# A mixture-of-experts kernel on one core: second-layer products on two row tiles

## The chip, the cores and the metric

The kernel runs on one core of a Trainium2 chip. Its time is the device time of one execution in microseconds. Before the change the median of three timed runs is 708.6 us (708.54 to 709.06).

## What is computed

The reference has two parts. The first is linear attention over 8 batches, 8 heads and 576 positions: features are exp(p) and exp(−p) of a projection less its largest magnitude, and out = (q · (k v)) / (q · z). The second part takes the attention's output as x, 4608 tokens of 512 numbers, and sends each token to one of 8 experts:

```python
for each token s of batch b, in order:
    fresh_e = argmax(logits[b, s])
    e = fresh_e if s == 0 or local_gate[b, s] < 0.5 else prev_e
    prev_e = e
    h = np.maximum(x[b, s] @ w1[e], 0.0)        # 512 -> 1024
    out[b, s] = p[e] * (h @ w2[e])              # 1024 -> 512, p is the softmax of the logits
```

Which expert gets which token is known only on the chip, so the kernel makes lists of tokens there.

## The kernel before, in words

The attention and the gates fill the first 280 us or so. What follows is the experts' work, in *slots*. A slot is one expert's weights and up to four *units* of 128 tokens. The order of the slots is fixed in `moe` and `slots`: two early slots of three units each, and then, from about 347 us, slots of four and of three units in turn (four of each), with one *two-expert slot* after the first two, then a slot of two units, and last the *late* slot, which again has two experts. A two-expert slot is one unit whose 128 rows are 64 tokens of one expert and 64 of another. In some slots the last unit is short (96 tokens); which ones is fixed too.

A slot has two layers. `layer1` multiplies the weights with x, 512 to 1024, for all the units at once, eight blocks of 128 features, each in four products over 128 inputs; ScalarE's ReLU writes `hh` and VectorE the remainder `hl` (L1433, L1434). `layer2` then goes unit by unit: eight blocks `f` of 128 features are the 128 rows of the contraction, the unit's tokens are the stationary operand and 512 columns of w2 stream past.

Numbers are split in two for the one-pass format fp32r: a high part and the low remainder, for the weights (`whi`, `wlo`: `split`, a cast on ScalarE at L1208 and a subtraction on VectorE at L1211) and for the activations. A product of two such numbers is three matmuls, high by high, high by low, low by high (`three`, L1387 to L1389). "A product" below is one such matmul: a unit's second layer has 8 × 3 = 24 of them, all added in one PSUM bank, tile `l2`, which has two buffers. Two-expert slots go through the other branch of `both` (L1400), which uses plain fp32 and two 128x64 column tiles, one for each expert.

When a unit is done, VectorE scales its rows by the gate's probability (L1499; ScalarE does it in the early slots, L1497) into `y`, which has two buffers, and POOL scatters the rows to the output with an indirect DMA (L1503, `put`). The late slot is finished by `last_rows`, in two parts of the columns. `halfbanks` gives the two-bank tile into which a two-expert slot turns rows (L1369); of two such tiles one was in the pool of `l2` with a name of its own, the other in a pool beside it.

The instructions of each engine stand in the order in which the program issues them, TensorE's exactly in the written order. While `layer2` runs, calls from `between` and `used`/`spare` issue the next slot's work between the blocks: weights are loaded by SyncE, split by ScalarE and VectorE, and the next x is turned and split into high and low parts. Splits of weights stand behind the last marked instruction of their engine (`past`, `marks`), and the scaling of a unit sets such a mark.

Of the kernel before, what the change touches and what calls it, by code (L numbers as in the profile page):

```python
# [7 lines left out]
F32 = mybir.dt.float32  # L8
# [5 lines left out]
ALU = mybir.AluOpType  # L14
# [5 lines left out]
DM, E, FF = 512, 8, 1024  # L20
# [46 lines left out]
class Kernel:  # L67
# [236 lines left out]
    def paced_load(self, at, behind):  # L304

        if self.loads and NBP * NHP * NC - 12 - len(self.loads) < at - 4:
            with self.tc.issue_after(behind.ins):
                self.loads.pop(0)()
# [958 lines left out]
    def halfbanks(self):  # L1267

        self.trn = getattr(self, "trn", 0) + 1
        return (self.psr if self.trn % 2 else self.pst).tile([128, 2, 512], F32, name="tr", bufs=1)  # L1270

    def into(self, s):
        if "x" not in s:
# [117 lines left out]
    def both(self, s, k, o, ah, al, c, first, last):  # L1391
# [6 lines left out]
        for z in (0, 1):  # L1398
            r = slice(64 * z, 64 * z + 64)
            self.last_pe = self.pe.matmul(o[r], ah.bitcast(F32)[:, r], w[z][:, c], start=first, stop=last)  # L1400

    def behind(self):

        x, self.last_num = self.last_num, None
        return self.tc.issue_after(x.ins) if x else nullcontext()
# [64 lines left out]
    def layer2(self, s, between, held=None):  # L1470
        dve = self.dve
        hh, hl = s["h"]
        self.need(s, 8) if len(s["ei"]) == 1 else None
        if held is not None:
            return self.last_rows(s, between, held)
        for k in range(s["n"]):
            if hasattr(self, "psr"):
                t = self.psr.tile([128, DM], F32, name="l2")
            else:
                t = self.psb.tile([128, DM], F32, name="l2", tag="nm")  # L1480
            o = self.unit(s, k)
            t = t[0:o.stop - o.start]
            for f in range(8):
                c = slice((f % 2) * DM, (f % 2) * DM + DM)
                self.both(s, 4 + f // 2, t, hh[:, f, o], hl[:, f, o], c, f == 0, f == 7)
                if f in ((0, 2) if s["n"] > 1 else (1, 3, 5)) and between:
                    between.pop(0)()
                if f % 2 and k == s["n"] - 1:
                    self.used(1)
                elif f % 2:  # L1490
                    self.spare()
            rows = slice(0, o.stop - o.start)
            y = self.mx2.tile([128, DM], F32, name="y")[rows]
            u = s["u"] + k
            prob = s["prob"][rows, u:u + 1]
            if s in self.eslots:
                self.marks[self.act] = self.act.mul(y, t, prob)  # L1497
            else:
                self.marks[dve] = dve.tensor_scalar_mul(y, t, prob)  # L1499
            self.put(y, s["tok"][rows, u:u + 1])  # L1500

    def put(self, y, at):
# [5 lines left out]
    def last_rows(self, s, between, held):  # L1508

        hh, hl = s["h"]  # L1510
        y = self.mx2.tile([128, DM], F32, name="y")
        u = s["u"]
        prob = s["prob"][:, u:u + 1]
        for a, b in ((0, WIDE), (WIDE, DM)):
            t = self.psr.tile([128, DM], F32, name="l2")[:, 0:b - a]
            for f in range(8):
                c = slice((f % 2) * DM + a, (f % 2) * DM + b)
                self.both(s, 4 + f // 2, t, hh[:, f], hl[:, f], c, f == 0, f == 7)
            self.marks[self.act] = self.act.mul(y[:, a:b], t, prob)
        self.used(4)  # L1520
        held.append(lambda at=s["tok"][:, u:u + 1]: self.put(y, at))
# [174 lines left out]
```

## Time and profile before

| | |
|---|---|
| median of the timed runs | 708.6 us |
| the profiled execution's own time | 705.87 us |
| its span, first to last instruction | 704.1 us |
| instructions in the trace | 21968 |
| TensorE busy | 696.7 us (99%) |
| TensorE loading weights (beside its matmuls) | 615.7 us (87%) |
| VectorE busy | 475.7 us (68%) |
| ScalarE busy | 351.0 us (50%) |
| POOL busy | 236.4 us (34%) |

Busy time is the union of the rows' durations. A matmul's end is modelled and matmuls overlap, so the pace of TensorE is read from the starts of rows that follow each other, and not from their durations. The profiled execution is one execution; the timed runs are others. In a row, `128*128` is the part of the array that is used (rows by columns), and `128x512` the streamed operand.

### The profile page before, as it was taken

What the parts mean: (1) busy time and instruction counts of PE and PEld (TensorE: products, weight loads), DVE (VectorE), ACT (ScalarE), POOL (GpSimd) and SP (SyncE); (2) the same over time, 40 slices, a digit from 0 to 9 for tenths busy, and PEclk for the clock granted to TensorE, in tenths of its full rate; (3) what the DMA queues carried; (4) which work ended last, traced back from release to release, by engine and by line L of the source; (5) the groups of instructions that cost most, each with busy time, mean ns of one, the idle gap of its engine ahead of it and who ended that gap; (6) DMA issues with size and microseconds to landing.
All of it is one profiled execution on the core that took longest, in us unless ns stands there. A gap on an engine that the chain in (4) does not pass through costs nothing. (4 is left out here: it accounts for less than half of the span.)

```text
span 704.1 us, 21968 instructions
## 1 busy us (share of the span) xinstructions
PE 696.7 (99%) x9193; PEld 615.7 (87%) x9193; DVE 475.7 (68%) x878; ACT 351.0 (50%) x696; POOL 236.4 (34%) x349
## 2 busy tenths in 40 slices
PE   8999999999999999999999999999999999999997
PEld 7999999999999999889888975889888997889894
DVE  6888899889998986694538348455756466644610
ACT  6667676766778884243534226342425143424320
POOL 0211101420257674665606053042523225140201
PEclk9999999999999999999999999999999999999999
DMA  8855545554578843254887998736866686646611
GB/s 241 257 159 151 160 129 147 150 148 138 143 226 247 265 142 92 56 192 147 281 190 256 343 331 316 165 143 173 216 184 186 193 185 215 152 148 154 242 55 41
DMA packets 100885, 129.51 MB, mean 184 GB/s; under 512 B 41682, under 2 KB 80018, under 8 KB 100734
## 3 DMA queue, kind: packets, MB, share of 16 engines
q1 hardware_dynamic: 92304, 105.10, 51.9%
q0 software_dynamic: 8032, 22.78, 9.7%
q8 instruction: 73, 1.20, 0.7%
q14 instruction: 28, 0.23, 0.1%
q10 hardware_dynamic: 448, 0.20, 0.1%
HBM read 98.12 MB, written 21.80 MB: 170 GB/s over the span
## 5 line engine op out<-in xcount | busy, mean ns | idle before, releaser
L1433 ACT ACTIVATE hh<-l 128x384 fp32r<-128x384 f32 (+4 forms) x88 | 45.0, 511 | 163.2 <-PE l L1389 163.0
L1387 PE MATMUL l<-xhi,whi 128*128 128x352 f32 (+5 forms) x352 | 124.2, 353 | 0.0
L1389 PE MATMUL l<-xhi,wlo 128*128 128x352 f32 (+5 forms) x352 | 123.6, 351 | 0.0
L1388 PE MATMUL l<-xlo,whi 128*128 128x352 f32 (+5 forms) x352 | 123.4, 351 | 0.0
L1434 DVE SCALAR_TENSOR_TENSOR hl<-l,hh 128x384 fp32r<-128x384 f32 (+4 forms) x88 | 51.0, 580 | 100.3 <-ACT hh L1433 100.2
L1211 DVE TENSOR_TENSOR wlo<-wraw,whi 128x1024 fp32r<-128x1024 f32 x80 | 101.8, 1289 | 23.2 <-ACT whi L1208 23.0
L1387 PE MATMUL l<-whi,hh 128*128 128x512 f32 (+1 forms) x288 | 112.7, 391 | 0.0
L1388 PE MATMUL l<-wlo,hh 128*128 128x512 f32 (+1 forms) x288 | 112.3, 390 | 0.0
L1389 PE MATMUL l<-whi,hl 128*128 128x512 f32 (+1 forms) x288 | 112.3, 390 | 0.0
L420 ACT ACTIVATE kp<-sb 128x512 f32<-128x512 f32 x140 | 81.1, 624 | 41.0 <-DVE sb L412 39.7
L410 DVE TENSOR_REDUCE m<-pj 128x8 f32<-128x1024 f32 x70 | 85.4, 1221 | 16.6 <-PE pj L407 12.9
L1208 ACT CAST whi<-wraw 128x1024 fp32r<-128x1024 f32 x80 | 82.0, 1045 | 18.4 <-PE l L1389 12.7
L412 DVE TENSOR_TENSOR sb<-pj,m 128x1024 f32<-128x1024 f32 x70 | 85.7, 1225 | 6.2 <-DVE m L410 0.5
L538 PE MATMUL nm<-kvs,qp 128*64 128x74 f32 x2304 | 86.9, 227 | 0.0
L407 PE MATMUL pj<-first,kq 64*128 64x128 f32 x1120 | 81.3, 285 | 0.3 <-ACT ks L508 0.3
L538 PEld LDWEIGHTS nm<-kvs,qp 128*64 128x64 f32 x2304 | 79.6, 136 | 0.4 <-issue 0.3
L443 ACT ACTIVATE qp<-pj 128x512 f32<-128x512 f32 x140 | 76.4, 597 | 6.6 <-PE pj L428 6.2
L460 PE MATMUL kvp<-v,kp 128*64 128x65 f32 x2048 | 77.1, 225 | 0.1
L1503 POOL DMA_INDIRECT out<-y,p_tokm x32 | 40.5, 1267 | 104.5 <-DVE y L1499 93.7
L407 PEld LDWEIGHTS pj<-first,kq 64*128 64x128 f32 x1120 | 67.9, 187 | 6.1 <-ACT ks L508 0.5
L1387 PEld LDWEIGHTS l<-xhi,whi 128*128 128x128 f32 x352 | 66.1, 188 | 6.7 <-issue 0.8
L1388 PEld LDWEIGHTS l<-xlo,whi 128*128 128x128 f32 x352 | 66.2, 188 | 5.4
(269 smaller groups left out, 977.0 us busy)
## 6 DMA issues: line engine op xcount, KB each, us to landing
wraw<-in_w1h SPq DMA_DIRECT2D x40, 512.0 KB
wraw<-in_w2h SPq DMA_DIRECT2D x40, 512.0 KB
kq<-in_kqT SPq DMA_DIRECT2D x88, 192.0 KB
v<-in_va SPq DMA_DIRECT2D x48, 195.0 KB
xs<-xo SPq DMA_DIRECT2D x48, 128.0 KB
whi<-in_w2h SPq DMA_DIRECT2D x8, 512.0 KB
wlo<-in_w2h SPq DMA_DIRECT2D x8, 512.0 KB
xs<-xo SPq DMA_DIRECT2D x16, 192.0 KB
```

The costliest lines, as they stand in the source:

```text
L407: self.last_pe = self.pe.matmul(t[:, h, i % 2, j, :], kq[r, j, s], self.w2[r], start=True, stop=True)
L410: dve.tensor_reduce(m, f, AX.X, ALU.max, apply_absolute_value=True)
L412: self.last_dve = dve.tensor_sub(sb.rearrange("p h c j f -> p (h c j) f"), f, m.unsqueeze(2).broadcast_to([128, 8, 128]))
L420: self.last_act = act.activation(kp[:, :, :, sg, :].rearrange("p c h f -> p h c f"), sb[:, :, :, 0], AF.Exp, scale=1.0 - 2 * sg)
L443: self.act.activation(qp[:, sg].rearrange("p h (c r k) -> p (h c) r k", c=2, r=2), src, AF.Exp, scale=1.0 - 2 * sg)
L460: self.last_sum = self.pe.matmul(t[r, sg, h], kp[:, h, sg, r], v[:, h], start=first and sg + h == 0, stop=last and sg + h == 2)
L538: self.last_num = self.pe.matmul(e["t"][r, c - c0, k], self.ch[i]["qp"][:, sg, h, q0 + r.start:q0 + r.stop], kvs[:, sg, k], start=sg == 0, ...
L1208: self.act.copy(hi, raw)
L1211: (low or self.dve).tensor_sub(lo[:, c], raw[:, c], hi.bitcast(F32)[:, c])
L1387: mm(o, ah, bh, start=first, stop=False)
L1388: mm(o, ah, bl, start=False, stop=False)
L1389: self.last_pe = mm(o, al, bh, start=False, stop=last)
```

## The change

The second layer of each slot with one expert, from the point where the late pools are open (so not in the two early slots), is computed by `row_tiles`. Each matmul of 128 rows becomes two of 64 rows: the lower half of the contraction goes to the first bank of a pair and the upper half to the second. The two banks of the pair are added when the rows are scaled: ScalarE multiplies the first bank by the probability into `y`, and VectorE multiplies the second and adds `y`. The tile `l2` is therefore two banks wide, still with two buffers, and the turn tile of `halfbanks` that stood in the same pool becomes one of these buffers. Two-expert slots use the first bank of such a tile and VectorE's scaling as before.

```diff
     def halfbanks(self):
         self.trn = getattr(self, "trn", 0) + 1
-        return (self.psr if self.trn % 2 else self.pst).tile([128, 2, 512], F32, name="tr", bufs=1)
+        if self.trn % 2:
+            return self.psr.tile([128, 2, 512], F32, name="l2")
+        return self.pst.tile([128, 2, 512], F32, name="tr", bufs=1)
...
+    def row_tiles(self, s, k, t, ah, al, c, first, last):
+
+        wh, wl = s["w"][k]
+        for a, b in ((ah, wh), (ah, wl), (al, wh)):
+            for r in (0, 1):
+                p = slice(64 * r, 64 * r + 64)
+                self.last_pe = self.pe.matmul(t[:, r], a[p], b[p, c], start=first and b is wh and a is ah,
+                                              stop=last and a is al)
...
         for k in range(s["n"]):
-            if hasattr(self, "psr"):
-                t = self.psr.tile([128, DM], F32, name="l2")
+            rest = hasattr(self, "psr")
+            split = rest and len(s["ei"]) == 1
+            o = self.unit(s, k)
+            rows = slice(0, o.stop - o.start)
+            if rest:
+                t = self.psr.tile([128, 2, DM], F32, name="l2")[rows]
             else:
-                t = self.psb.tile([128, DM], F32, name="l2", tag="nm")
-            o = self.unit(s, k)
-            t = t[0:o.stop - o.start]
+                t = self.psb.tile([128, 1, DM], F32, name="l2", tag="nm")[rows]
             for f in range(8):
                 c = slice((f % 2) * DM, (f % 2) * DM + DM)
-                self.both(s, 4 + f // 2, t, hh[:, f, o], hl[:, f, o], c, f == 0, f == 7)
+                if split:
+                    self.row_tiles(s, 4 + f // 2, t, hh[:, f, o], hl[:, f, o], c, f == 0, f == 7)
+                else:
+                    self.both(s, 4 + f // 2, t[:, 0], hh[:, f, o], hl[:, f, o], c, f == 0, f == 7)
...
-            if s in self.eslots:
-                self.marks[self.act] = self.act.mul(y, t, prob)
+            if split:
+                self.marks[self.act] = self.act.mul(y, t[:, 0], prob)
+                self.marks[dve] = dve.scalar_tensor_tensor(y, t[:, 1], prob, y, ALU.mult, ALU.add)
+            elif s in self.eslots:
+                self.marks[self.act] = self.act.mul(y, t[:, 0], prob)
             else:
-                self.marks[dve] = dve.tensor_scalar_mul(y, t, prob)
+                self.marks[dve] = dve.tensor_scalar_mul(y, t[:, 0], prob)
             self.put(y, s["tok"][rows, u:u + 1])
...
-            t = self.psr.tile([128, DM], F32, name="l2")[:, 0:b - a]
+            t = self.psr.tile([128, 2, DM], F32, name="l2")[:, 0, 0:b - a]
```

## Rows read from the trace of the kernel before

**Rows 1.** The page: busy us, share and instructions by engine; granted clock in 40 slices.

```profile
PE 696.7 (99%) x9193; PEld 615.7 (87%) x9193; DVE 475.7 (68%) x878; ACT 351.0 (50%) x696; POOL 236.4 (34%) x349
...
PEclk9999999999999999999999999999999999999999
```

**Rows 2.** Busy time by stage: the slots after the early ones; one second layer.

```profile
core 0: us, PE busy (x) PEld busy (x) DVE busy (x) ACT busy (x) POOL busy (x), PEclk, DMA share, GB/s
346.94:691.86 344.92, 344.92 (x1698) 290.08 (x1696) 186.99 (x226) 123.95 (x190) 101.64 (x84) 1.00 0.69 202
...
458.42:480.18 21.76, 21.76 (x98) 18.02 (x96) 13.55 (x15) 7.09 (x9) 9.96 (x8) 1.00 0.40 131
```

**Rows 3.** Timeline, second layer of four full units: start us, us, engine, line, operation.

```profile
458.42 0.39 PE L1387 MATMUL l<-whi,hh 128*128 128x512 f32 x1
...
478.14 0.39 PE L1387 MATMUL l<-whi,hh 128*128 128x512 f32 x1
478.14 0.19 PEld L1388 LDWEIGHTS l<-wlo,hh 128*128 128x128 f32 x1
...
480.18 0.32 PE L1387 MATMUL l<-xhi,whi 128*128 128x352 f32 x1
```

**Rows 4.** Timeline, first layer of the two-unit slot, 96 products, to the next layer.

```profile
666.78 0.30 PE L1387 MATMUL l<-xhi,whi 128*128 128x320 f32 x1
...
680.86 0.39 PE L1387 MATMUL l<-whi,hh 128*128 128x512 f32 x1
```

**Rows 5.** Timeline, a short unit's 24 products, between a full unit and the next slot.

```profile
506.30 0.39 PE L1389 MATMUL l<-whi,hl 128*128 128x512 f32 x1
506.53 0.39 PE L1387 MATMUL l<-whi,hh 128*96 128x512 f32 x1
...
512.05 0.39 PE L1387 MATMUL l<-xhi,whi 128*128 128x512 f32 x1
```

**Rows 6.** Groups by line and shape: the scaling (xcount | busy us, mean ns | idle before).

```profile
L1499 DVE TENSOR_SCALAR y<-l,p_probm 128x512 f32<-128x512 f32 x27 | 20.1, 746 | 37.8 <-PE l L1389 37.8
...
L1499 DVE TENSOR_SCALAR y<-l,p_probm 96x512 f32<-96x512 f32 x4 | 3.0, 740 | 1.5 <-DMA out<-y,p_tokm 1.5
```

**Rows 7.** Timeline, the attention's plain fp32 row tiles: twelve matmuls and the next.

```profile
102.75 0.84 PE L407 MATMUL pj<-first,kq 64*128 64x128 f32 x12
103.42 0.22 PE L428 MATMUL pj<-first,sb 64*128 64x64 f32 x1
```

**Rows 8.** Timeline, TensorE into and out of the two-expert slot's column tiles.

```profile
421.14 0.40 PE L1389 MATMUL l<-whi,hl 128*96 128x512 f32 x1
421.47 0.43 PE L1400 MATMUL l<-whi,xhi 128*64 128x256 f32 x1
...
435.52 0.59 PE L1400 MATMUL l<-whi,hh 128*64 128x512 f32 x1
...
435.95 0.59 PE L1400 MATMUL l<-whi,hh 128*64 128x512 f32 x1
...
436.48 0.50 PE L1387 MATMUL l<-xhi,whi 128*128 128x512 f32 x1
```

**Rows 9.** Groups by line and shape: weight splits, ReLU remainder, early slots' scaling.

```profile
L1211 DVE TENSOR_TENSOR wlo<-wraw,whi 128x1024 fp32r<-128x1024 f32 x80 | 101.8, 1289 | 23.2 <-ACT whi L1208 23.0
L1208 ACT CAST whi<-wraw 128x1024 fp32r<-128x1024 f32 x80 | 82.0, 1045 | 18.4 <-PE l L1389 12.7 <-DMA wraw<-in_w2h 2.8 <-DMA wraw<-in_w1h 2.8
L1434 DVE SCALAR_TENSOR_TENSOR hl<-l,hh 128x512 fp32r<-128x512 f32 x24 | 16.6, 692 | 32.0 <-ACT hh L1433 32.0
L1497 ACT ACTIVATE y<-l,p_probe 128x512 f32<-128x512 f32 x6 | 4.1, 686 | 7.1 <-PE l L1389 4.8 <-issue 2.3
```

**Rows 10.** Who waited for whom: us in total, times, longest.

```profile
POOL out L1503 <- DVE y L1499: 93.7, 17, 18.6
```

**Rows 11.** Timeline, the last scaling before the late slot, and the last scatter.

```profile
691.96 0.75 DVE L1499 TENSOR_SCALAR y<-l,p_probm 128x512 f32<-128x512 f32 x1 [4.69 <-PE l L1389]
...
699.67 0.97 POOL L1503 DMA_INDIRECT out<-y,p_tokm  x1 [5.71 <-ACT y L1519]
```

More of the change, by code (lines that the diff above doesn't have):

```diff
@@ L1491, in layer2 @@
                     self.spare()
-            rows = slice(0, o.stop - o.start)
             y = self.mx2.tile([128, DM], F32, name="y")[rows]
```

## The prediction

> **What bounds the kernel now.** I read the page first, then the busy times by stage, then single matmuls in order of time. The page shows TensorE busy for 99% of the span, at the full granted clock (the 2.4 GHz level) in all 40 slices [rows 1]. An average can hide a stage with another limit, so I looked at the part that the change touches: from 346.94 us, where the first slot after the two early ones starts, to 691.86 us TensorE is busy in 344.92 of 344.92 us, while VectorE has work for 187.0 and ScalarE for 124.0 [rows 2]. A busy TensorE is not yet one at its peak, since a matmul's row is longer than the distance to the next. So the pace has to be taken from starts. The second layer of a four-unit slot starts its 96 products at 458.42 and the next stage starts at 480.18: 226.7 ns for each product of 512 columns [rows 3]. The first layer of the two-unit slot starts 96 products of 320 columns at 666.78 and ends at 680.86: 146.7 ns each [rows 4]. The difference, 80.0 ns for 192 columns, is 0.417 ns for a column, one cycle of 2.4 GHz. So 512 columns stream in 213.3 ns and 13.3 ns are left over, the same at 320 columns (146.7 − 133.3). Short units of 96 tokens pace at 230 ns (24 products from 506.53 to 512.05), with 16.7 ns left over [rows 5]. This remainder is all that a change in the shape of the tiles can win; the streamed columns stay.
>
> **What is changed, and how much of it.** There are 31 scalings at L1499, 27 of full units and 4 of short ones [rows 6]; one full one belongs to the two-expert slot, which stays. So 26 full and 4 short units change, with 24 products each: 624 at 226.7 ns (141.5 us) and 96 at 230 ns (22.1 us). Every product becomes two, each on half of the rows, with the same 512 columns.
>
> **The pair against the product it replaces.** The trace has no one-pass product (the fp32r ones, one cycle a column) on half of the rows, so this is bounded by neighbours. Row tiles in plain fp32 stand in the attention: 12 matmuls, six pairs, from 102.75 to 103.42, 111.7 ns a pair for 128 columns [rows 7]. The two cycles a column of that form make 106.7 ns, so the two tiles do run together and 5 ns are left over for a pair. That bounds the new pair at the good end: 213.3 + 5 = 218.3 ns. The bad end, short of the tiles not running together, is that each of the two pays the remainder in turn: 213.3 + 2 × 13.3 = 240 ns. I take 226.7 (230 for short units), no change, and this is the choice on which the prediction hangs. My reason: with both tiles always occupied, a tile's next product follows its own last one, not the other tile's. Whatever costs 13.3 ns between two one-pass products in one place costs it again in each half, at the same time in both; a second tile hides a gap of the first only if it has spare time to fill, and here it has none. The fp32 rows show a small remainder, but they show it for a form that takes two cycles a column, so they don't say that the height of the tile makes it small. By this the 720 products cost 0, with −6.3 us (624 × 8.4 + 96 × 11.7 ns) and +9.3 us (720 × 13.3 less 96 × 3.3 ns, as a short pair would also be at 240) as the ends.
>
> The Trainium skill speaks against a gain too: in "TensorE: Matmul & The Clock Gate", section "Why this matters for your kernels", it says that a single matmul over few rows takes the same time as over 128, and that the gain lies in tiles at work together. No run here shows that for the one-pass form; by it the sum is the one I take.
>
> **Switches of the tiling.** Where the tile's shape changes, the trace has a gap. From short units to 128x64 tiles the step is 0.33 us where 0.23 is usual; from 128x64 tiles back to the full array it is 0.53 where 0.43 is [rows 8]. So a switch costs 0.10 us, both ways. A change between 128 and 96 columns of weights has none (506.30 to 506.53 is 0.23) [rows 5]. Nine slots go through the new second layer: four of four units, four of three and one of two. Each goes in and out, less the two that are switches already (before the two-expert slot and before the late one), so 16 are new: 1.6 us, all on TensorE and so on the path. They can hardly be hidden; they could be cheaper if fewer products were in flight, down to 1.0 us at 0.06.
>
> **The rows are scaled by two engines.** Before, VectorE scaled a unit in 746 ns. Now ScalarE does the first bank (686 ns in the early slots) and VectorE multiplies and adds the second (692 ns, by L1434, which has a PSUM and an SBUF input too) [rows 6, 9]. ScalarE gets 30 × 0.69 = 20.7 us more of 345 in which it now works 124; VectorE saves 1.6 us [rows 2]. Both lie beside TensorE's work: a unit lasts 24 × 0.227 = 5.4 us, the pairs of banks are two, and a pair must be free only one unit later, so 5.4 us are there for 1.4 us and the queues ahead of it. The longest entry that could stand ahead is a weight cast of 1.05 us or a split of 1.29 us [rows 9]. On ScalarE, casts and ReLUs queue behind the scaling while it waits for the unit's last product; the x parts for the next slot are wanted only after the last unit, and a slot's second layer leaves VectorE some 8 of 21.8 us idle [rows 2]. Without that cover a unit would cost up to 1.4 us, 42 us in all; I take 0. The scatter of the rows starts 0.7 us later and POOL waits anyway: 93.7 us for the scaling [rows 10]. The turn tile that moves into the same two pairs takes a pair free since the second-last unit: 0.
>
> **The end.** The last slot is a two-expert one and keeps its 128x64 tiles; the last scaled rows before it come at 691.96, 7.7 us ahead of the last scatter at 699.67 [rows 11]. The end moves with TensorE, by the sum.
>
> **Sum.** 0 + 1.6 + 0 + 0 = +1.6 us on the profiled execution's 705.87 (span 704.1), 707.5. That execution is 2.7 us under the median of the timed runs, 708.6, so I carry the difference over: 710.2 us. The case's own range is pairs from 226 to 230: 709.7 to 712.3.
>
> **Rivals.**
> - *The remainder belongs to the full height or to weight loads on busy rows, and goes (faster).* For it: the fp32 row tiles have only 5 ns. Pairs at 218.3 give −6.3 + 1.6 = −4.7 us, 703.9; with no remainder at all −9.9 + 1.6, 700.3. It decides as soon as a pair is under 224 ns. Against it: the load of the next weights starts in the same hundredth of a microsecond as the matmul on the same rows (478.14) and takes 0.19 of the 0.23 us, so it is already beside the work [rows 3]. The skill's same page, section "Part 3: Packing small matmuls", has the rule that would bring this: weights load beside a running matmul only where the rows differ. The trace does not bear it out here, for the reason just given.
> - *Each half pays in turn (slower).* Two loads of 128 columns and two starts for a product share one queue. Pairs at 240 ns: +9.3 + 1.6 = +10.9, 719.5. Against it: the fp32 pairs take four instructions in 111.7 ns.
> - *The tiles don't run together in the one-pass form*, which moves four bytes a column and cycle, twice the rate of the fp32 rows. Then the change doesn't do what it says: 720 × 227 = +163 us, 873. Against it: the columns read for each partition stay what they are now.
>
> **How the numbers follow.** A measurement tells about 0.2%, 1.4 us, from no change. No change in pace 0.44, of which 0.26 ends above 710.0 and 0.18 within; the remainder goes 0.37, all faster; in turn, or partly so, 0.12; not together 0.05; the rest, 0.02, to no difference. So faster 0.37, same 0.20, slower 0.43. The range is 701.8 to 716.5: it takes in the first rival but for its far end, the forecast, and half of the second.
>
> **What would show it.** Starts of the pairs in a second layer: 226 to 228 ns apart, with the two halves within 0.01 us of each other; steps of 0.32 us at the sixteen switches; ScalarE about 21 us busier; no idle TensorE before a unit. Pairs at 216 to 220 ns make it wrong and the kernel faster; 240 or more, wrong the other way. A wait of matmuls for the scaling would show the banks as the bound.

## The result: 6.8 us slower, and the profile after

The changed kernel takes 715.41 us (median of 4 runs, 714.38 to 715.95), the kernel before beside it 708.57. The ratio is 1.0093 (95% interval 1.0076 to 1.0111). The forecast was 710.2 in a range of 701.8 to 716.5, with "slower" the likeliest sign. So the sign was right, and 5.2 of the 6.8 us were not in the sum.

| | before | after |
|---|---|---|
| profiled execution's own time, us | 705.87 | 714.38 |
| span, us | 704.1 | 712.6 |
| instructions | 21968 | 23457 |
| first late-phase slot to late slot, us | 344.92 | 351.68 |
| of it, up to the 512-column first layer | 89.54 | 93.07 |
| of it, from there to the late slot | 255.38 | 258.61 |

The last three lines are the cleanest measure, since what stands ahead of 347 us differs by some us from one execution to the next, whatever the kernel (the same stretch starts at 346.94 in the profiled execution of before and at 348.19 in that of after). Of before, they go from 346.94 to 436.48 and on to 691.86 [rows 2, 8]. Their difference is 6.76 us, close to the 6.84 of the medians. The two spans differ by 8.5: in this execution 1.25 us more stand ahead of that start, and 0.5 more follow the start of the late slot (712.6 − 699.87 us, for 704.1 − 691.86). The page of the changed kernel, against [rows 1]:

```profile
PE 702.3 (99%) x9913; PEld 619.8 (87%) x9913; DVE 475.8 (67%) x878; ACT 369.5 (52%) x726; POOL 233.8 (33%) x349
...
PEclk9999999999999999999999999999999999999999
```

TensorE has 720 more matmuls, as counted, still at the full granted clock. ScalarE is 18.5 us busier and has 30 more instructions. The busy times by stage, against [rows 2] (us, then busy time of each engine with its instructions, clock, DMA share, GB/s):

```profile
core 0: us, PE busy (x) PEld busy (x) DVE busy (x) ACT busy (x) POOL busy (x), PEclk, DMA share, GB/s
348.19:699.87 351.68, 349.55 (x2417) 293.49 (x2415) 188.25 (x226) 142.54 (x220) 102.46 (x83) 1.00 0.67 198
441.26:699.87 258.61, 258.61 (x1778) 222.33 (x1776) 136.50 (x169) 104.31 (x163) 70.62 (x57) 1.00 0.58 170
348.19:441.26 93.07, 90.94 (x641) 71.16 (x639) 51.75 (x57) 38.23 (x57) 31.84 (x26) 1.00 0.91 277
...
463.25:485.26 22.01, 22.01 (x193) 17.94 (x193) 12.91 (x15) 9.04 (x12) 9.98 (x8) 1.00 0.37 118
```

Two different things are to be seen. In the later stretch TensorE is busy for 258.61 of 258.61 us and still takes 3.23 us longer than before: something costs time while it is "busy". In the earlier one it is idle for 2.13 us where before it was never idle. So there are two main causes, and each is followed to its instructions.

**Busy, and slower.** The timeline of a four-unit second layer, from its first layer into it and from it into the next slot, TensorE's matmuls (start us, us, operation; `x2` is a pair of row tiles):

```profile
462.71 0.39 PE L1390 MATMUL l<-xlo,whi 128*128 128x512 f32 x1
462.94 0.39 PE L1391 MATMUL l<-xhi,wlo 128*128 128x512 f32 x1
463.25 0.50 PE L1410 MATMUL l<-whi,hh 64*128 64x512 f32 x2
463.59 0.40 PE L1410 MATMUL l<-wlo,hh 64*128 64x512 f32 x2
...
484.94 0.39 PE L1410 MATMUL l<-whi,hl 64*128 64x512 f32 x2
485.26 0.43 PE L1389 MATMUL l<-xhi,whi 128*128 128x352 f32 x1
485.53 0.32 PE L1390 MATMUL l<-xlo,whi 128*128 128x352 f32 x1
485.69 0.32 PE L1391 MATMUL l<-xhi,wlo 128*128 128x352 f32 x1
```

and its weight loads at the second of these places:

```profile
485.26 0.19 PEld L1389 LDWEIGHTS l<-xhi,whi 128*128 128x128 f32 x1 [0.35 <-issue]
485.37 0.19 PEld L1390 LDWEIGHTS l<-xlo,whi 128*128 128x128 f32 x1
485.53 0.19 PEld L1391 LDWEIGHTS l<-xhi,wlo 128*128 128x128 f32 x1
```

Between switches the pairs are 0.23 apart, as the products were: (484.94 − 463.59) / 94 is 227.1 ns, where 226.7 stood in [rows 3]. At a switch two steps are long. The last product of the old shape lasts 0.31 or 0.32 us instead of 0.23: that is the 0.10 of the prediction. And the first product of the new shape lasts 0.34 instead of 0.23 (0.27 instead of 0.16 with 352 columns): 0.11 more. In the steady state a product's weight load starts when the product before it starts (both at 485.53), and the product follows 0.16 behind its load (485.69). Behind a switch the second load starts 0.11 late (485.37 behind 485.26), and the second product again follows 0.16 behind it. A switch costs 0.20 us by these rows. The trace of before has the long first product too, where [rows 8] end at 436.48; its next row is 0.34 us later:

```profile
436.82 0.40 PE L1388 MATMUL l<-xlo,whi 128*128 128x512 f32 x1
```

The Trainium skill names the first half only: "TensorEngine Tiling (Array Packing)", section "Key Properties", says that a change of the tiling mode drains the engine. The trace agrees, with 0.09 us; the other 0.11 follows the drain.

**Idle.** Who released TensorE after idle time in the changed kernel (us in total, times, longest), and the first of the two places on the timeline:

```profile
PE l L1410 <- DVE y L1513: 2.0, 2, 1.0
```

```profile
379.88 0.39 PE L1410 MATMUL l<-whi,hl 64*128 64x512 f32 x2
381.29 0.50 PE L1410 MATMUL l<-whi,hh 64*128 64x512 f32 x2 [1.02 <-DVE y L1513]
381.63 0.39 PE L1410 MATMUL l<-wlo,hh 64*128 64x512 f32 x2
```

From 379.88 to 381.29 are 1.41 us instead of 0.23. The second place is 386.66 to 388.02, 1.36 us; together 2.3 us too long. Unit 2 of the first four-unit slot wants the pair of banks that unit 0 filled by about 374.7 us, 5.4 us earlier, and VectorE had not scaled it by then. VectorE's timeline of the changed kernel and, in the fence behind it, ScalarE's:

```profile
376.32 4.25 DVE L1211 TENSOR_TENSOR wlo<-wraw,whi 128x1024 fp32r<-128x1024 f32 x3 [0.26 <-ACT whi L1208]
380.50 0.74 DVE L1513 SCALAR_TENSOR_TENSOR y<-l,p_probm,y 128x512 f32<-128x512 f32 x1
```

```profile
375.25 2.95 ACT L1208 CAST whi<-wraw 128x1024 fp32r<-128x1024 f32 x3
378.10 0.68 ACT L1512 ACTIVATE y<-l,p_probm 128x512 f32<-128x512 f32 x1
```

The same unit in the kernel before, on VectorE:

```profile
373.38 0.75 DVE L1499 TENSOR_SCALAR y<-l,p_probm 128x512 f32<-128x512 f32 x1
...
375.39 4.32 DVE L1211 TENSOR_TENSOR wlo<-wraw,whi 128x1024 fp32r<-128x1024 f32 x3
```

The operations and their lengths are the same. Their order is not: before, the scaling stood ahead of the run of three splits; after, it stands behind three casts on ScalarE and three splits on VectorE. Unit 1's scaling stands behind two more splits (383.43 to 387.23), which makes the second wait. The scaling's own price was as forecast on ScalarE, 686 ns, and 747 on VectorE, where the forecast had 692.

The first pair behind this wait lasts 0.34 us too (381.29 to 381.63), with the second weight load 0.11 behind the first, and here the shape stays the same:

```profile
381.29 0.19 PEld L1410 LDWEIGHTS l<-whi,hh 64*128 64x128 f32 x2 [1.45 <-DVE y L1513]
381.40 0.19 PEld L1410 LDWEIGHTS l<-wlo,hh 64*128 64x128 f32 x2
```

By these rows the second half of a switch's price is that of a restart, with or without a change of shape. The full array shows it too, behind a wait in `pair_banks_behind` (595.21 to 595.55).

**A small third loss.** The two-expert slot takes 15.36 us, for 15.01 before. One product of its first layer starts 0.51 us behind the one before it (429.20 to 429.71), not 0.22. It is released by a ReLU on ScalarE, and ScalarE's new scaling, that of the last unit of the slot before (428.70, 0.68 us), stands in front of that ReLU (429.29). Who released TensorE's weight load there:

```profile
PEld l L1402 <- ACT hs L1474: 0.6, 1, 0.6
```

### The profile page after: what moved, and what is told of

Same layout as the page of the kernel before. It is cut to its first block, busy times and chain, and to the rows that moved or that the text cites. A ratio compares the mean times of both kernels' runs of the same rounds, so it can differ in the third digit from the quotient of the medians.

```text
span 712.6 us, 23457 instructions
## 1 busy us (share of the span) xinstructions
PE 702.3 (99%) x9913; PEld 619.8 (87%) x9913; DVE 475.8 (67%) x878; ACT 369.5 (52%) x726; POOL 233.8 (33%) x349
## 3 DMA queue, kind: packets, MB, share of 16 engines
q8 instruction: 79, 1.29, 0.8%
## 5 line engine op out<-in xcount | busy, mean ns | idle before, releaser
L1410 PE MATMUL l<-whi,hh 64*128 64x512 f32 (+1 forms) x480 | 96.4, 392 | 2.0 <-DVE y L1513 2.0
L1410 PE MATMUL l<-whi,hl 64*128 64x512 f32 (+1 forms) x480 | 95.4, 387 | 0.0
L1410 PE MATMUL l<-wlo,hh 64*128 64x512 f32 (+1 forms) x480 | 95.2, 387 | 0.0
L1521 POOL DMA_INDIRECT out<-y,p_tokm x32 | 43.2, 1350 | 104.4 <-DVE y L1513 84.8
L1391 PEld LDWEIGHTS l<-xhi,wlo 128*128 128x128 f32 x352 | 66.1, 188 | 5.4
```

What stands on the lines that cost most here:

```text
L1391: self.last_pe = mm(o, al, bh, start=False, stop=last)
L1410: self.last_pe = self.pe.matmul(t[:, r], a[p], b[p, c], start=first and b is wh and a is ah, stop=last and a is al)
```

## Experiments

Eleven kernels. Each one's profiled execution was cut at the same two places, the start of the 512-column first layer (about 440 us) and that of the late slot. "Later stretch" is the time between them, 255.38 us in the kernel before. Each ratio is to executions of the kernel before that were timed beside it (medians 707.90 to 708.57 us).

| kernel | us | ratio to before (95%) | later stretch | new switches in it |
|---|---|---|---|---|
| the change | 715.41 | 1.0093 (1.0076–1.0111) | 258.61 | 13 |
| `pair_banks` | 710.58 | 1.0033 (1.0022–1.0044) | 255.37 | 0 |
| `pair_banks_behind` | 708.53 | 1.0007 (0.9998–1.0016) | 255.97 | 0 |
| `three_pairs` | 714.21 | 1.0101 (1.0085–1.0116) | 258.60 | 13 |
| `one_scaling` | 714.39 | 1.0089 (1.0074–1.0103) | 258.61 | 13 |
| `every_other_unit` | 718.29 | 1.0152 (1.0137–1.0166) | 261.82 | 26 |
| `lower_half_alone` | 711.41 | one run; before 708.38 | 257.98 | 13 |
| `all_row_tiles` | 715.03 | 1.0101 (1.0083–1.0118) | 255.34 | 0 |
| `forms_full_array` | 723.63 | one run; before 708.38 | not comparable | 0 |
| `splits_aside` | 717.68 | 1.0135 (1.0118–1.0152) | 258.65 | 13 |
| `splits_behind` | 715.00 | 1.0109 (1.0092–1.0126) | 258.94 | 13 |
| `all_row_tiles_behind` | 714.48 | 1.0088 (1.0067–1.0109) | 255.40 | 0 |

### Two banks without row tiles: `pair_banks`

```diff
-                    self.row_tiles(s, 4 + f // 2, t, hh[:, f, o], hl[:, f, o], c, f == 0, f == 7)
+                    self.both(s, 4 + f // 2, t[:, f // 4], hh[:, f, o], hl[:, f, o], c, f % 4 == 0, f % 4 == 3)
```

> Full-array products as before, but the first four blocks go to one bank of a pair and the last four to the other, and both engines scale and add as in the change. No new switch of the tile shape. Theory A (switches of the tile shape at 0.20 us each and late scalings of the first slot make the change slow): only the late scalings can be left, 708.6 plus 0 to 2.3, so 708.6 to 710.9. Rival B (the two-engine scaling and its load on ScalarE cost most): 713 or more.

It cost 2.3 us. The wait at unit 2 is there and the later stretch is as before; behind the start of the late slot the trace is 0.5 us longer, as in the change:

```profile
PE l L1389 <- DVE y L1513: 1.3, 1, 1.3
```

So the wait doesn't need row tiles, and the switches do.

### Twice as many switches: `every_other_unit`

```diff
-            split = rest and len(s["ei"]) == 1
+            split = rest and len(s["ei"]) == 1 and k % 2 == 0
```

> Row tiles only in the first, third, ... unit of a slot, the others as before: half the pairs, but 33 new switches in place of 16. Theory A: 33 x 0.20 = 6.6 us over before, plus up to 1.2 for one late scaling, 715.2 to 716.4. Rival C (the loss is in the pairs, not in the switches): half of the change's loss, 712. By the forecast's 0.10 us for a switch: 708.6 + 3.3 = 711.9.

Of the 30 units 17 keep their row tiles, and the kernel is slower: 718.29 us. Its later stretch (same columns as above):

```profile
442.18:704.00 261.82, 261.56 (x1538) 218.06 (x1537) 139.66 (x171) 100.11 (x156) 69.90 (x57) 1.00 0.60 170
```

That is 6.44 us over before, 0.43 of it one wait, with 26 new switches: 0.23 us each. The change itself has 3.23 us with 13: 0.25 each. The number of switches sets this part, not the number of row tiles. The time is 1.9 us above the range that was expected: a switch costs more than 0.20 in this stretch, and three scalings come late in the earlier one, not one.

### One of the two tiles: `lower_half_alone`

```diff
-            for r in (0, 1):
+            for r in (0,):
...
-                self.marks[self.act] = self.act.mul(y, t[:, 0], prob)
-                self.marks[dve] = dve.scalar_tensor_tensor(y, t[:, 1], prob, y, ALU.mult, ALU.add)
+                self.marks[dve] = dve.tensor_scalar_mul(y, t[:, 0], prob)
```

> The change with the lower half of each product alone: one 64x128 tile works, the other stands still, and the upper half of the contraction is left out of the output. It asks what the 13.3 ns between products hang on. If they belong to a stream of one-pass products on whatever tile (my reason in the forecast): 227 ns from start to start, as the pair and the full product have. If the height of the tile or loads on busy rows make them: 213 to 220 ns. If a second tile at work was what kept the pair slow: also 213 to 220. The time is near one_scaling's, 712 to 715, in the first case, and some 5 us lower in the others.

A half-height product alone goes at the pace of the pair. Its timeline in the same second layer:

```profile
461.44 0.49 PE L1410 MATMUL l<-whi,hh 64*128 64x512 f32 x1
461.77 0.39 PE L1410 MATMUL l<-wlo,hh 64*128 64x512 f32 x1
...
483.13 0.39 PE L1410 MATMUL l<-whi,hl 64*128 64x512 f32 x1
483.44 0.43 PE L1389 MATMUL l<-xhi,whi 128*128 128x352 f32 x1
```

(483.13 − 461.77) / 94 is 227.2 ns, the pair's 227.1. So the second tile is free, and half the height saves nothing: the remainder stands in each tile, with or without a neighbour. The later stretch is 2.60 us longer with 13 switches, 0.20 each, as in the rows. The time, one execution, is under the 712 to 715 that were expected: the two waits are not there, and 3.0 us for sixteen switches are left.

### No switches: `all_row_tiles`

The first layer of the late slots runs on row tiles too, into a pair of banks of which only the first is read (the upper half of the first layer's contraction is not added).

```diff
+                        for a, b in ((wh, xh), (wh, xl), (wl, xh)):
+                            for r in (0, 1):
+                                p = slice(64 * r, 64 * r + 64)
+                                self.last_pe = self.pe.matmul(t[:, r, 0:w1], a[p, c], b[p, d, :], ...)
...
-                        self.three(t[:, j, :], wh[:, c], wl[:, c], xh[:, d, :], xl[:, d, :], d == 0, d == 3)
```

> Row tiles in the first layer too (after the early slots), so that the shape of the tiles hardly changes any more: one new switch in place of 16. The first layer's upper half goes to a second bank that is left out of the output; the turn tile beside the sums is given up. Theory A: 708.3 + 0.2 for the switch + 0.5 for the pairs + 2.3 for the late scalings of the first slot = 711.3, and no steps between the layers. Rival C (the pairs or their instructions cost, not the switches): twice as many pairs, so twice the loss that is left without the waits, 708.3 + 8 + 2.3 = 718.

The time, 715.03, was not the 711.3 expected, but the stretch that was to tell is clean:

```profile
444.02:699.36 255.34, 255.34 (x2451) 219.08 (x2449) 136.91 (x170) 104.35 (x163) 70.21 (x57) 1.00 0.60 173
```

255.34 us, where before has 255.38: with every matmul of it cut in two and no change of shape, the whole of the 3.23 us is gone. What kept the time up are waits in the earlier stretch, three now and longer:

```profile
PE l L1407 <- DVE y L1518: 4.3, 3, 2.1
```

Three of its four timed executions also have a mean granted clock of 0.995 or 0.996, where the kernel before has 0.998 to 1.000; see `all_row_tiles_behind` below.

### The form of the product: `forms_full_array`

In the two-unit slot of the kernel before, unit 0 uses plain fp32 and unit 1 bf16 constants (its result is not the product).

```diff
+        if form == F32:
+            ah, al, bh, bl = [x.bitcast(F32) for x in (ah, al, bh, bl)]
+        elif form == BF16:
+            ah = al = self.ones_b
+            bh = bl = self.ones_b.unsqueeze(1).broadcast_to([128, 4, 128])
```

> The kernel before, but in the slot of two units the first unit's 24 products take the same operands as plain fp32, and the second unit's 24 products are bf16 products of constant ones (128x128 on 128x512), so the output of that slot is not the reference's. If the remainder belongs to the one-pass fp32r form: plain fp32 on the full array at 427 + 2 to 5 ns for each of its two instructions, bf16 at 214 to 219 ns. If it belongs to the full height of the array: 427 + 13 = 440 ns, and 227 ns. The time is 24 x (854 - 227) ns = 15 us over before.

Full-height products of 512 columns, first fp32 (two rows for each), then bf16:

```profile
683.70 1.02 PE L1393 MATMUL l<-whi,hh 128*128 128x512 f32 x2
...
704.30 0.38 PE L1393 MATMUL l<-consts 128*128 128x512 bf16 x1
...
709.31 0.38 PE L1395 MATMUL l<-consts 128*128 128x512 bf16 x1
```

fp32 takes 858 ns a product ((704.30 − 683.70) / 24), 4 × 213.3 + 5; bf16 takes 217.8 ((709.31 − 704.30) / 23), 213.3 + 4.5. So at full height, on busy rows, the remainder is 5 ns in these forms and 13.3 in fp32r. It belongs to the form. That answers the one piece of the trace that spoke for the faster rival, the 5 ns of the fp32 row tiles [rows 7]. Whether the streaming of fp32r or its weight loads make the 13.3 ns (0.19 us a load, 0.10 in bf16) isn't separated here.

### Whose order makes the waits: `one_scaling`, `three_pairs`, `splits_aside`

`one_scaling`: VectorE alone scales the first bank; the second is not added.

```diff
-                self.marks[self.act] = self.act.mul(y, t[:, 0], prob)
-                self.marks[dve] = dve.scalar_tensor_tensor(y, t[:, 1], prob, y, ALU.mult, ALU.add)
+                self.marks[dve] = dve.tensor_scalar_mul(y, t[:, 0], prob)
```

> Row tiles as in the change, but VectorE alone scales the first bank, as before, and the upper half of the contraction is left out of the output. Theory A: the 16 switches (3.2 us) and the pairs stay, and VectorE's scaling of the first unit still stands behind three weight splits, so 713 to 715. Rival B: without ScalarE in the scaling the time goes back by most of the loss, to 710 or less.

```profile
PE l L1410 <- DVE y L1512: 2.0, 2, 1.0
```

The same two waits, without ScalarE in the chain. VectorE's scaling still stands behind the three splits (4.25 us). Put beside `pair_banks` and `lower_half_alone` this says when the order turns: with 48 matmuls a unit and one operation it is turned, with 24 and two operations too, with 24 and one it is as before (and that kernel has no such wait). Either half of the change, the doubled matmuls or the second operation, is enough. Why the order comes out so, when the program is built, was not tried.

`three_pairs`: a third pair of banks for `l2`, without the separate turn tile.

```diff
-        self.psr = self.mkpool(root, "moe_ps3", 2, "left", PSUM)
+        self.psr = self.mkpool(root, "moe_ps3", 3, "left", PSUM)
```

> The change with a third pair of banks for the sums (the turn tile beside them is given up and takes its turn in the three). Theory A: the two waits of TensorE in the first slot (1.18 and 1.13 us) go, everything else stays: 715.4 - 2.3 = 713.1, and the steps at the switches stay 0.2 us. Rival B (ScalarE and VectorE are simply behind in each slot): the waits move to a later unit and the time stays at 715.

```profile
PE l L1386 <- DVE hl L1442: 1.4, 1, 1.4
```

The two waits are gone, as they should be when a pair is free one unit later, but VectorE is late all the same, and the next slot's first layer waits 1.4 us for a ReLU remainder queued behind a scaling. The traced stretch up to the late slot is 1.2 us shorter than the change's (350.51 for 351.68); the timed ratio can't be told from the change's.

`splits_aside`: POOL does two of the splits.

```diff
-            self.split(self.loaded.pop(0))
+            self.split(self.loaded.pop(0), self.pool if aside > 0 else None)
```

> The change with two of the weight splits of the first slot's first unit on POOL in place of VectorE (2 x 1.2 us less ahead of the scaling). Theory A (VectorE is behind in the first slot, by the splits that stand ahead of the scaling): the two waits of TensorE go or nearly so, 715.4 - 2 = 713.4, and the scaling of the first unit ends before 380 us. Rival D (ScalarE's casts make it late): the waits stay, 715.4.

```profile
PE l L1391 <- DVE hl L1447: 3.6, 2, 3.4
...
PE l L1412 <- DVE y L1517: 0.6, 1, 0.6
```

Worse, and both times that were expected are missed. With two splits off VectorE the scaling of unit 0 ends at 379.93 us and unit 2 no longer waits; but unit 3 waits 0.6 us, and a longer wait stands in the next slot. VectorE and POOL in that kernel:

```profile
379.83 3.04 POOL L1211 TENSOR_TENSOR wlo<-wraw,whi 128x256 fp32r<-128x256 f32 x3
...
382.18 3.74 DVE L1211 TENSOR_TENSOR wlo<-wraw,whi 128x1024 fp32r<-128x1024 f32 x2
385.84 0.74 DVE L1517 SCALAR_TENSOR_TENSOR y<-l,p_probm,y 128x512 f32<-128x512 f32 x1
```

POOL needs about 1 us for a quarter of a split (3.04 for three), and the scaling of unit 1 still stands behind two splits on VectorE, 3.74 us. The splits were moved, not the order, so this run settles nothing on the order alone.

### The order alone: `splits_behind`, `pair_banks_behind`, `all_row_tiles_behind`

In units 0 and 1 of a slot, splits that fall due are written behind the unit's scaling.

```diff
+            self.hold = split and k < 2
...
-        while len(self.loaded) > keep:
+        while len(self.loaded) > keep and not getattr(self, "hold", False):
...
+            if getattr(self, "hold", False):
+                self.hold = False
+                self.landed(3 if hasattr(self, "ml1") else 2)
```

> The changed kernel, with one difference of order: in units 0 and 1 of every one-expert slot the weight splits that fall due during the unit (cast on ScalarE, subtraction on VectorE) are written behind that unit's scaling and not ahead of it. Nothing is added or left out. In the trace of the changed kernel the two waits of TensorE in the first 4-unit slot (gaps of 1407 and 1358 ns, 2.3 us over the usual pace) stand behind a scaling that came after three casts (2.95 us) and three splits (4.25 us). Theory A, the order alone makes these two waits: they are gone, the slot's second layer takes about 22.1 us (16.5 + 5.6) and not 24.6, and the time is 715.4 - 2.3 = 713.1 us, with the switches' part, from the 512-column first layer to the late slot, as it was (258.6 us). Theory B, VectorE has no room for it in any order: the splits come late for the next slot, a wait of about 1.4 us stands there in its place, as in the kernel with three pairs of banks, and the time is 714 to 715.4. Theory C, the waits come from the banks themselves: they stay, 715.4.

> The kernel with full-array products whose blocks 0 to 3 and 4 to 7 go to two banks, scaled by both engines, with the same difference of order: splits of units 0 and 1 are written behind the unit's scaling. It has no switch of the tile shape. It measured 710.58 against 708.26 us with its one wait of 1.3 us over the pace and every other stage as before. Theory A, the second bank and the second engine cost nothing but the wait that the order makes: the wait is gone, region from the first late-phase slot to the late slot 344.9 us as before, ratio 1.000 (0.999 to 1.0015). Theory B, the scaling in two steps has a price of its own wherever it stands: a wait of 0.7 to 1.6 us is still there, in this slot or the next, ratio 1.001 to 1.003.

> The kernel whose first-layer products run on row tiles too (the second bank of the first layer is left out of the sum, so its output is not the reference's), with the same difference of order. In the run without it three waits of TensorE for a scaling stood, 1.41 + 1.10 us in the first 4-unit slot behind splits and 2.28 us in the 3-unit slot behind copies of gathered rows; all other stages together were 0.5 us above before. Theory A, switches and waits are all there is: the first two waits are gone, 715.03 - 2.5 = 712.5 us, or 710.3 if the copies also fall behind the scaling, and the stretch from the 512-column first layer to the late slot is 255.3 us as it was and as in the kernel before (255.4). Theory B, row tiles have a cost of their own per product beside the switches: with the waits gone that stretch is over 256 us.

The changed kernel in this order no longer waits in the first four-unit slot (its second layer takes 22.1 us, as expected), but once, 0.7 us, in the next:

```profile
PE l L1410 <- DVE y L1514: 0.7, 1, 0.7
```

Its profiled execution takes 350.25 us from the first late-phase slot to the late one, 1.43 less than the change, but the timed median is 715.00 (713.89 to 717.27) and the interval covers the change's. The 713.1 that was expected is missed, and 715.00 lies in the range of the rival, in which a wait in the next slot takes the place of the two. So the trace shows that the order makes these two waits, and the timed runs show no gain. Two of the five timed executions, 715.00 and 717.27, have a mean granted clock of 0.995, the other three (713.89 to 715.15) 0.999 or 1.000, and the change's four 0.998 or 0.999. Those two were not traced; what such a loss can look like stands under `all_row_tiles_behind`.

In `pair_banks` the timed runs do show it: 710.58 becomes 708.53, 1.0007 (0.9998 to 1.0016), no difference from before that can be told. Two banks, added by two engines, then cost at most 1.1 us by that interval. In its trace the two places that are left are one wait of 0.3 us in a later slot (that stretch is 0.6 us longer than before) and the time behind the start of the late slot, 0.4 us longer.

`all_row_tiles_behind` lost the two waits and got a longer third, 5.4 us. Copies of gathered rows stand ahead of the scaling there, and the first of them waits for its DMA. Rows of VectorE and TensorE:

```profile
419.10 1.54 DVE L1345 COPY xz<-xg 128x1024 uint16<-128x1024 uint16 x2 [11.52 <-DMA xg<-xz]
...
421.99 0.75 DVE L1519 SCALAR_TENSOR_TENSOR y<-l,p_probm,y 128x512 f32<-128x512 f32 x1
...
422.79 0.74 PE L1407 MATMUL l<-whi,hh 64*96 64x512 f32 x2 [5.38 <-DVE y L1519]
423.33 0.62 PE L1407 MATMUL l<-wlo,hh 64*96 64x512 f32 x2
423.76 0.63 PE L1407 MATMUL l<-whi,hl 64*96 64x512 f32 x2
```

And this wait costs more than its length. TensorE's last pair ahead of it starts at 417.02. While TensorE stands idle its granted clock falls from the 2.4 to the 1.2 GHz level: it is 1.00 from 418 to 420 us, 0.60 on average from 420 to 422, 0.50 from 422 to 426, and 1.00 again from 428. The ten pairs from 422.79 to 427.17 are therefore 0.44 us apart and not 0.23, 2.1 us more. The mean clock of this execution is 0.993. Three of the four timed ones have 0.993 or 0.994 and take 713.56 to 715.88 us; the fourth, at 1.000, takes 712.30, near the 712.5 that was expected.

Its later stretch, 255.40 us, is that of before a second time: row tiles in themselves neither cost nor give anything there.

## Why the prediction was right in its sign and short in its size

- **The pace of the pairs (0): right, and for the reason given.** 227.1 ns for 226.7. The remainder stands in each tile (`lower_half_alone`, 227.2) and belongs to fp32r (`forms_full_array`). The rival in which it goes, held at 0.37, and the one in which the halves pay in turn are both refuted by the starts; the tiles run together.
- **"So a switch costs 0.10 us, both ways": mis-sized, and the first failing step.** It costs 0.20 us in the rows and 0.20 to 0.25 over a stretch. The trace at hand showed the second half. The new shape starts at 436.48 [rows 8] and its second product at 436.82; I read only the step into the new shape. The 0.06 allowed as a cheaper switch stands in no row. Sixteen at 0.10 made 1.6 us; the later stretch alone, with 13, lost 3.23. Of the difference between 0.20 and 0.25 a switch, some 0.4 us are in the 448-column first layer, which takes 20.03 us instead of 19.45: its products start 207 ns apart all along, where before it was 203, so this is no part of the switch. Why stays open.
- **"The longest entry that could stand ahead is a weight cast of 1.05 us or a split of 1.29 us": wrong, and the second failing step.** Three of each stood ahead, 2.95 and 4.25 us, and the cover of 5.4 us was gone. I took the order of the trace of before as given, but the change turned it. By stage, the first four-unit slot's second layer took 24.6 us (369.08 to 393.71) where it had taken 21.8, and of these 2.8 us 2.3 are the two waits. That the order makes them is shown (`splits_behind`, `pair_banks_behind`). The prediction named such a wait as the sign of the banks as the bound; the banks are enough when the scaling is in time.
- **ScalarE's longer queue, put at 0.** It delayed one ReLU, and TensorE with it, by 0.3 us in the two-expert slot. ScalarE became 18.5 us busier, for about 21.
- **The end: right for TensorE, and 0.5 us short.** The late slot starts 6.76 us later against the first late-phase slot, and the last scatter starts 7.8 us behind that start, as before. But from that start to the end of the trace are 12.7 us and not 12.2. It is 12.2 in the traces in which one engine scales the last unit ahead of the late slot (`one_scaling`, `lower_half_alone`, `every_other_unit`) and 12.7 in all the traces with two. What in those last microseconds takes longer was not tried.
- **The sum.** 3.23 in the later stretch; 3.53 in the earlier, of which 2.3 are the waits, 0.2 the two restarts behind them, 0.6 to 0.75 three more switches, 0.35 the two-expert slot (15.36 us from 425.90, for 15.01 before). Forecast: 1.6 for all. Of the signs that "would show it", no idle TensorE before a unit is the one that failed outright.
- **The range: luck.** 715.41 lies under the upper bound, 716.5, only because that bound left room for halves that pay in turn, which the starts refute. The case's own range, 709.7 to 712.3, does not hold it. The sign came from the switches, and they do cost time.

How much of the waits stands in the executions that were timed and not traced is open: `splits_behind` takes 1.4 us off the traced execution and nothing measurable off the median. The lower mean clock in two of its five executions fits longer waits there, which is argued and not shown.

No kernel here beats the one before; the best is `pair_banks_behind`, which can't be told from it.

## What to carry to other kernels

Price a change of shape by stepping over it in the trace until the pace is back, on both sides: the last product of the old shape and the first of the new. When cover is counted in queue entries, ask what can gather ahead in that queue, not which entry is longest, and expect a change of the operations to turn the order in which the program issues them. Cutting a product into row tiles doesn't touch a remainder that each tile pays for its own next product.

## What the runs showed of the hardware that was not expected

Behind a change of tile shape the second weight load starts 0.11 us late, so the first product lasts 0.34 us for 0.23; behind a wait with no change of shape it is the same. In a wait of 5.4 us the granted clock fell to the 1.2 GHz level while TensorE was idle, and the ten pairs that followed took 2.1 us more (`all_row_tiles_behind`). The remainder over one column a cycle is 13.3 ns a product in fp32r, 4.5 in bf16 and 5 in plain fp32 (for four passes), all on the full array. One half-height tile alone and two side by side keep the same pace, 227 ns for 512 columns.
